# Linear attention and an ELU feed-forward layer on one core: the first two batches' k maxima by one strided reduction each pair of slots, the first batch's attention slot by slot, and new orders of work for the head and the first two blocks

## The chip, the core and the metric

The kernel runs on one core of one Trainium2 chip. The metric is the device time of one execution in microseconds (us). A core has a matrix engine (TensorE, PE in the profile; its weight loads are listed as PEld), a vector engine (VectorE, DVE), a scalar engine (ScalarE, ACT), a general one (GpSimd, POOL) and a queue engine (SyncE, SP) which here only issues transfers. Each engine works through its own instructions in the order in which the program wrote them, and waits on semaphores for the others.

## The reference

```
q_s = exp(q - max(q, axis=-1));  q_s /= sum(q_s, axis=-1)         # over the 64 columns of a row
k_s = exp(k - max(k, axis=2));   k_s /= sum(k_s, axis=2)          # over the 576 positions
kv  = einsum('bhsd,bhse->bhde', k_s, v)
att = einsum('bhsd,bhde->bhse', q_s, kv)
x   = att.transpose(0, 2, 1, 3).reshape(4608, 512)
h   = x @ w_in                                                    # 512 -> 2048
g   = where(h > 0, h, exp(min(h, 0)) - 1)
out = g @ w_out                                                   # 2048 -> 512
```

q, k and v have 8 batches, 8 heads, 576 positions and 64 columns, in float32.

## The kernel before

**Blocks and steps.** Block j (0 to 7) takes the feed-forward layer of 512 positions of batch j; the 64 positions that are left of each batch are gathered into a ninth block of 512. A block has 16 steps, one for each chunk of 128 of the 2048 hidden columns. A step issues `hidden` (four matmuls of 128x512, L912, then ACT's exponential L895 or, in some chunks, the clipped form L892 and L893, then POOL's affine step L896), then the projection (`project`, four matmuls L933 of the chunk three steps back, LAG = 3), then `elu` on DVE (L925). Hidden results use three PSUM banks in turn (the first four chunks use a fourth), the projection four others, and one bank (AB) is left for attention. So PE alternates four L912 and four L933.

**Attention as words.** While block j runs, the attention of batch j + 1 is done in small pieces. Each piece is a word; a table gives, for each step, three strings of words: behind `hidden`, behind `project`, behind `elu`. FIRST is the table of block 0, SECOND of block 1, LATER and CHANGED of the rest. What comes ahead of block 0, batch 0's whole attention with the first loads, is one string, START. The order in a string is the order in which instructions enter their engines' queues, and so an order written by hand. Words used below: `load:Q:1:A` (a transfer, on SP unless an engine is named), `qmax`, `qsub`, `qexp`, `qsum`, `qmul` (softmax of q: L672, L679, L684, L689/L691, L708), `kmax` (maximum of k over the positions that a partition holds, L326 in the first two batches), `kturn` and `kacross` (transposes by matmul and the maximum across partitions, L331, L358), `diag` and `kspread` or `kraw`/`kmin` (the maxima put on a diagonal by ACT, L368, and spread or subtracted by matmul, L465, L513, L524), `ksub` (L438), `kexp`, `vconv` (v to bf16), `kv` (L560), `kfac` (scale by the sums of k), `pturn`/`pwide` (transposes of q, L766, and their copy), `att`/`xc` (L805 and the copy into XT, the transposed input of block's hidden matmuls), `w1:a:b`, `w2:a:b` (weight chunks a to b-1, issued by POOL: L255, L262), `h` (hidden matmuls of block 0 in START), `warm` (matmuls of ones, L1093). `kout` and `kin` (L423) bring later batches' maxima through a scratch tensor in DRAM into NB, on ACT's queue. `hold` makes SP wait for the latest hidden matmul.

**Slots.** In batches 0 and 1 a slot is a pair of heads with nine rows of 64 columns in each partition (QN = 9); a slot's load of q, k or v has 288 KB, and there are four. `kmax_first` takes the maximum of the nine rows with four `tensor_tensor` instructions of DVE by way of KT2: rows 0 to 3 against 4 to 7, then 2 against 2, then 1 against 1, then row 8. `kturn_first`, `kacross_first` and what follows work on halves A (slots 0, 1) and B (2, 3); so do, in batch 0, `vconv_first`, `kv_first`, `kv_fac`, `qturn_slots` and `qwide_first`.

Keys of the semaphores are strings in `op`; a word waits for the writers of the keys that it reads.

Of the kernel before, what the change touches and what calls it, by code (L numbers as in the profile page):

```python
# [38 lines left out]
AT = {"rawA": 0, "rawA2": 1, "rawB": 7, "rawB2": 4, "rawS": 3, "rawT": 2,  # L39
      "kturnA": 4, "kturnB": 5, "kvA": 6, "kvB": 4, "pturnA": 5, "pturnB": 5,  # L40
      "att0": 6, "att1": 2, "att2": 3, "att3": 4, "clip": (1, 2, 4, 6, 8, 10, 11, 17, 21, 30, 32, 33, 37, 42, 44)}
START = ("load:Q:0:1 load:K:0:0 load:K:0:1 warm:1:7 warm:4:7 qmax:1 warm:2:4 load:Q:0:3 qsub:1:dve "
# [3 lines left out]
         "w1:4:6 kacross:B kexp:S vconv:A:act kmin:A qsub:2:gp qsub:3:gp diag:act:B w2:2:3 qsum:0 kmin:B "  # L46
         "kexp:A load:V:0:3 kmin:T qexp:2 qmul:A:dve qsum:2 load:V:0:2 qexp:3 w1:6:9 "
         "qsum:3 vconv:B:gp load:K:1:M qmul:2:gp kexp:B kexp:T kv:A kfac:A:dve pturn:A kv:B "
         "pwide:A:act kfac:B:act warm:1:3 att:1 att:0 qmul:3:gp pturn:B xc:1:dve xc:0 h:2:4 "
         "pwide:B:act w2:3:4 att:2 att:3 xc:2 load:Q:1:A load:Q:1:R w2:4:6 h:0:2 xc:3 kmax2:AB ")  # L50
FIRST = {
    0: ("qmax:A ksub:R:dve", "", "qsub:0:dve"),
    1: ("w1:13:14", "w1:9:12", "qsub:1:dve"),
    2: ("", "qmax0:R", "w2:6:9"),
    3: ("hold qexp:A", "load:Q:1:B:act", ""),
    4: ("w1:12:13", "w2:9:13", "load:K:1:R qsum:A qsub0:R:dve"),
    5: ("w1:14:16", "kturn", "kacross vconv:R qmax:C"),
    6: ("", "qmul:A hold", "load:V:1:RAB"),
    7: ("qexp0:R", "", "diag qsub:2:dve"),
    8: ("qsub:D", "kspread load:K:2:MR copy ksub:1 qsum0:R", "qexp:C qmulr0:dve ksub:0 qsum:C"),  # L60
    9: ("pturn:A", "", "ksub:3 kexp:R qmul:B:dve pwide:A:act"),
    10: ("", "pturn0:R pwide0:R:act", "ksub:2:dve vconv:A:gp"),
    11: ("rest0 rcopy0:act", "kexp:A", ""),
    12: ("pturn:B w2:15:16", "pwide:B:act load:Q:2:ABR", "w2:13:15"),
    13: ("kv:A vconv:B:dve", "kfac:A:dve", "kexp:B peak2:B att:0 xc:0"),
    14: ("kv:B kfac:B:dve peak2:R qmulr:gp", "att:1 peak2:A", "join2 turn:R xc:1"),
    15: ("att:3", "xc:3", "att:2 load:V:2:MR xc:2 kout2"),
}
SECOND = {
    0: ("qmax:C qsub:D", "", "qmax:A"),  # L70
    1: ("", "qsub:1 wide0:R:dve", ""),
    2: ("", "qsub:0 load:K:2:MR", ""),
    3: ("kin", "qsub:2 qexp:A", "qsum:A vconv:A:gp"),
    4: ("", "", "ksub:A"),
    5: ("rest0", "qexp:C", "peak2:B"),
    6: ("ksub:3:dve rcopy0:act vconv:B", "ksub:R:dve", "load:Q:2:MR"),
    7: ("", "kexp:A", "ksub:2 kexp:R"),
    8: ("qmul:1 qsum:C qmul:0:dve", "vconv:R", "kexp:B qmulr:dve"),
    9: ("turn:A", "qmul:B:dve", ""),
    10: ("peak2:R wide:A:gp kv:AB", "", ""),  # L80
    11: ("kfac:AB:dve", "turn:R turn:B qmax2:A", ""),
    12: ("peak2:A wide:R:act", "flat:0", "xflat:0:act"),
# [38 lines left out]
class Gen:  # L121
# [976 lines left out]
    def first_batch(self):  # L1098
# [7 lines left out]
        for word in START.split():  # L1106
# [101 lines left out]
```

## Time and profile before

| | us |
|---|---|
| time, median of 3 runs | 310.69 (310.32 to 311.09) |
| span of the profiled execution | 308.1 |
| PE busy | 297.6 (97%) |
| first L912 (hidden matmul) | 19.88 |
| first L933 (projection) of block 0 | 24.47 |
| of block 1 | 61.56 |
| of block 2 | 94.26 |
| of block 3 | 125.52 |

The times are of whole executions; the profile is of one execution, for which the page gives its span, 308.1 us, from the first to the last instruction. Times of events are counted from the span's start. The first L933 of a block is used as a mark, since PE alternates L912 and L933 from there on, and the distances between such marks show in which block time is spent.

### The profile page before, as it was taken

The numbers are of one execution on the slowest core, as the hardware profiler recorded it, in microseconds if no ns is written. First come the engines' busy times: TensorE is split into PE (matmuls) and PEld (weight loads), VectorE is DVE, ScalarE is ACT, GpSimd is POOL, SyncE is SP. The second block draws the span as 40 slices with busy tenths as digits, with TensorE's granted clock in tenths as the row PEclk, the third lists the DMA queues.
The fourth block names the chain that finished last, engine by engine and source line by source line (L and its number), as shares of the span: only waits on it lengthen the run. The fifth ranks groups of instructions, "written<-read, shape, count | busy, mean of one in ns | idle before, by whom it ended". The sixth has DMA issues, their size and how long they took to land.

```text
span 308.1 us, 4839 instructions
## 1 busy us (share of the span) xinstructions
PE 297.6 (97%) x1733; PEld 240.1 (78%) x1733; DVE 235.0 (76%) x400; ACT 192.9 (63%) x358; POOL 171.3 (56%) x215
## 2 busy tenths in 40 slices
PE   7789899999999999999999999999999999999995
PEld 4467677788878888888888888888888888888884
DVE  6988978979959897999889988998895353335442
ACT  2678975577559784877587758775877543334432
POOL 2968873686436743786278637863686333333440
PEclk9999999999999999999999999999999999999999
DMA  7999999985708993768475846590512030003004
GB/s 261 393 340 364 372 345 257 273 253 145 191 3 246 261 251 105 223 122 231 133 217 144 208 143 209 146 198 3 172 23 57 2 136 0 0 2 136 0 0 136
DMA packets 60584, 51.63 MB, mean 168 GB/s; under 512 B 26897, under 2 KB 50705, under 8 KB 60561
## 3 DMA queue, kind: packets, MB, share of 16 engines
q1 hardware_dynamic: 52960, 41.23, 47.7%
q0 software_dynamic: 6400, 8.39, 10.5%
q10 hardware_dynamic: 1200, 1.72, 2.0%
q8 instruction: 13, 0.21, 0.3%
q14 instruction: 11, 0.08, 0.1%
HBM read 38.27 MB, written 9.45 MB: 155 GB/s over the span
## 4 chain that ended last, share of the span: by engine, by line
PE 85%; DMA 6%; POOL 4%; ACT 2%; DVE 2%; issue 1%
PE bank L933 40%; PE bank L912 40%; DMA W2S<-in_moe_w_out_dram 5%; PE bank L827 2%; POOL W1S L255 1%; PE bank L598 1%; DMA QR<-in_q_dram 1%; POOL QR L679 1%; POOL QS L708 1%; PE bank L805 1%; DVE KT L326 1%; DVE QF L672 0%; PE bank L560 0%; ACT ES L895 0%; ACT ES L893 0%
## 5 line engine op out<-in xcount | busy, mean ns | idle before, releaser
L933 PE MATMUL bank<-W2S,GT 128*128 128x512 f32 x572 | 153.4, 391 | 1.4 <-DMA W2S<-in_moe_w_out_dram 1.2
L896 POOL TENSOR_SCALAR ES<-ES 128x512 f32<-128x512 f32 (+1 forms) x130 | 85.8, 662 | 117.3 <-ACT ES L895 117.3
L912 PE MATMUL bank<-XT,W1S 128*128 128x512 f32 x512 | 138.4, 392 | 0.5 <-issue 0.3
L925 DVE SCALAR_TENSOR_TENSOR GT<-bank,ES 128x512 fp32r<-128x512 f32 (+1 forms) x130 | 87.9, 681 | 54.4 <-PE bank L912 40.6
L933 PEld LDWEIGHTS bank<-W2S,GT 128*128 128x128 f32 x572 | 106.3, 188 | 23.6 <-DMA W2S<-in_moe_w_out_dram 1.6
L895 ACT ACTIVATE ES<-bank 128x512 f32<-128x512 f32 (+1 forms) x130 | 76.0, 592 | 70.9 <-PE bank L912 70.7
L912 PEld LDWEIGHTS bank<-XT,W1S 128*128 128x128 f32 x512 | 94.1, 188 | 19.9 <-ACT XT L814 0.9
L679 POOL TENSOR_TENSOR QR<-QR,QM 128x512 f32<-128x512 f32 (+1 forms) x21 | 24.9, 1187 | 0.6 <-DVE QM L672 0.5
L684 ACT ACTIVATE QR<-QR 128x1024 f32<-128x1024 f32 (+3 forms) x19 | 19.0, 1006 | 3.1 <-DVE QR L679 3.1
L855 ACT ACTIVATE XT<-bank 128x320 fp32r<-128x320 f32 (+1 forms) x30 | 15.0, 501 | 9.4 <-PE bank L827 9.3
L689 DVE TENSOR_REDUCE QZ<-QR 128x16 f32<-128x1024 f32 (+1 forms) x14 | 18.8, 1343 | 0.6 <-ACT QR L684 0.6
L672 DVE TENSOR_REDUCE QM<-QR 128x16 f32<-128x1024 f32 (+1 forms) x14 | 18.8, 1342 | 0.0
L912 PE MATMUL bank<-XTR,W1S 128*128 128x512 f32 x64 | 16.6, 389 | 0.0
L438 DVE TENSOR_TENSOR KR<-KR,NB 128x512 f32<-128x512 f32 x16 | 14.6, 938 | 0.0
L623 ACT ACTIVATE MB<-bank,KZ 64x64 fp32r<-64x64 f32 x44 | 10.1, 302 | 7.0 <-DVE KZ L614 6.9
L387 DVE TRANSPOSE_TENSOR_REDUCE KM<-KR 128x32 f32<-128x1024 f32 x12 | 14.4, 1226 | 0.0
L857 POOL CAST QT<-QW 128x1024 fp32r<-128x1024 f16 x12 | 12.5, 1039 | 2.9 <-DMA QW<-QS 2.9
L912 PEld LDWEIGHTS bank<-XTR,W1S 128*128 128x128 f32 x64 | 12.0, 188 | 2.5
L892 ACT ACTIVATE ES<-bank 128x512 f32<-128x512 f32 x15 | 8.9, 594 | 7.9 <-PE bank L912 7.9
L827 PE MATMUL bank<-QT,MB 128*128 128x320 f32 (+1 forms) x48 | 12.5, 300 | 0.7 <-ACT XT L855 0.7
L708 POOL TENSOR_TENSOR QS<-QR,QI 128x1024 f16<-128x1024 f32 (+1 forms) x7 | 12.5, 1783 | 0.4 <-DVE QI L691 0.4
L484 ACT ACTIVATE EK<-KR 128x1024 bf16<-128x1024 f32 x12 | 12.6, 1050 | 0.0
(108 smaller groups left out, 262.8 us busy)
## 6 DMA issues: line engine op xcount, KB each, us to landing
out_dram<-OSB SPq DMA_DIRECT2D x30, 256.0 KB, 2.7
KR<-in_k_dram SPq DMA_DIRECT2D x6, 1024.0 KB, 7.7
VR<-in_v_dram SPq DMA_DIRECT2D x6, 1024.0 KB, 6.3
QR<-in_q_dram SPq DMA_DIRECT2D x5, 1024.0 KB, 8.0
KR<-in_k_dram SPq DMA_DIRECT2D x8, 288.0 KB, 6.1
VR<-in_v_dram SPq DMA_DIRECT2D x8, 288.0 KB, 6.6
W1S<-in_moe_w_in_dram POOLq DMA_DIRECT2D x3, 768.0 KB, 9.2
QR<-in_q_dram SPq DMA_DIRECT2D x4, 512.0 KB, 11.2
```

The lines of the kernel that those rows point to most:

```text
L672: self.op("dve", lambda: v.tensor_reduce(m, QR, AX.X, ALU.max), self.qkeys(b, part), self.qstat("QM", b, part))
L679: self.op(en, lambda: e.tensor_tensor(QR, QR, m, ALU.subtract), keys + self.qstat("QM", b, part), self.qown(b, part))
L684: self.op("act", lambda: a.activation(QR, QR, AF.Exp), keys, self.qown(b, part))
L689: self.op("dve", lambda: v.tensor_reduce(z, QR, AX.X, ALU.add), self.qkeys(b, part), self.qstat("QZ", b, part))
L708: self.op(en, lambda: e.tensor_tensor(out, QR, z, ALU.mult), keys + self.qstat("QI", b, part), [f"QS{x}" for x in cells])
L827: last = pe.matmul(self.bank[bank][:, a - c0:b - c0], self.MB[f][:, :, :].rearrange("p u d -> p (u d)"), self.QT[:, f, a - f * S:b - f * S ...
L855: self.op("act", lambda: e.activation(out, src, AF.Copy), reads, writes)
L895: self.op("act", lambda: a.activation(ES[:, x], ps[:, x], AF.Exp), [f"bank{bank}"], keys + mark)
L896: self.op("gp", lambda: g.tensor_scalar(ES[:, x], ES[:, x], -1.0, 1.0, ALU.add, ALU.mult), keys, keys)
L912: return pe.matmul(ps, self.W1S[:, kc, c * 128:(c + 1) * 128], x[:, kc, 0:SM], start=(kc == 0), stop=(kc == 3))
L925: self.op("dve", lambda: v.scalar_tensor_tensor(out[:, x], *how), [f"bank{bank}"] + eks + (["FINE"] if n < FINE else []), keys)
L933: return pe.matmul(self.bank[OB[t]][:, :], self.GT[n % NG][:, t * 128:(t + 1) * 128], self.W2S[:, c, :], start=(c == 0), stop=(c == NCH - ...
```

## The change

Four parts:

1. `kmax_first` is one `tensor_reduce` (maximum over the innermost axis) on a view of k in which the nine rows are the innermost axis, with a step of 64 elements (256 bytes). One instruction takes two slots: 128x128 out of 128x1152. KT2 goes.
2. Batch 0 works per slot from q's product on: `vconv`, `kv`, `kfac`, `pturn`, `pwide` and `att` take a slot (0 to 3) or a half; the keys QT and VF are split by slot (`cells`, `slots`), and each slot has its own banks (`kv0` to `kv3`, `pturn0` to `pturn3`). `pwide` of a slot goes through the common `copy`.
3. START, FIRST and SECOND are written anew. In START the k loads come first, W1's chunks 0 to 3 are one transfer instead of two, all 16 hidden matmuls of the first four chunks are there, slice by slice (`h:kc:c0:c1`), and `hidden` issues none for them. Batch 1's q loads A and R go over POOL's queue instead of SP's. In FIRST, `kturn`, `kacross`, `diag`, `kspread` and `copy` stand in step 5 (before: steps 5 to 8). In SECOND, `kin` goes from step 3 to 4, and its first user, `ksub:A`, from POOL behind step 4 to DVE in step 5.
4. In `program`, the store of a finished block stands ahead of the words of that step, not behind them.

```diff
-START = ("load:Q:0:1 load:K:0:0 load:K:0:1 warm:1:7 warm:4:7 qmax:1 warm:2:4 load:Q:0:3 qsub:1:dve "
-         "load:Q:0:0 kmax:0 warm:3:5 load:K:0:2 kraw:A qexp:1 kmax:1 load:K:0:3 kturn:A load:V:0:1 "
-         "qmax:0 kraw:S qsum:1 qsub:0:gp kacross:A load:Q:0:2 kmax:3 kraw:B kmax:2 kmax2:R "
-         "load:V:0:0 w1:1:4 w1:0:1 diag:act:A qmax:2 kmin:S qexp:0 kraw:T kturn:B w2:0:2 qmax:3 "
-         "w1:4:6 kacross:B kexp:S vconv:A:act kmin:A qsub:2:gp qsub:3:gp diag:act:B w2:2:3 qsum:0 kmin:B "
-         "kexp:A load:V:0:3 kmin:T qexp:2 qmul:A:dve qsum:2 load:V:0:2 qexp:3 w1:6:9 "
-         "qsum:3 vconv:B:gp load:K:1:M qmul:2:gp kexp:B kexp:T kv:A kfac:A:dve pturn:A kv:B "
-         "pwide:A:act kfac:B:act warm:1:3 att:1 att:0 qmul:3:gp pturn:B xc:1:dve xc:0 h:2:4 "
-         "pwide:B:act w2:3:4 att:2 att:3 xc:2 load:Q:1:A load:Q:1:R w2:4:6 h:0:2 xc:3 kmax2:AB ")
+START = ("warm:10:2 load:K:0:1 load:K:0:0 load:Q:0:0 kmax:A kraw:S qmax:0 qsub:0:gp qexp:0 load:K:0:3 kturn:A kacross:A "
+         "w1:0:4 kraw:A load:K:0:2 load:Q:0:1 diag:dve:A load:Q:0:2 load:V:0:0 kmin:A kmax:B kmin:S kturn:B "
+         "load:Q:0:3 qmax:1 kexp:A vconv:0:act qmax:2 kraw:T kacross:B load:V:0:3 qsub:1:gp qmax:3 kexp:S "
+         "kraw:B load:V:0:1 qsub:2:gp qsum:0 diag:act:B qsub:3:gp qmul:0:gp kmin:T qexp:1 qsum:1 kv:0 "
+         "qexp:2 vconv:1:act qexp:3 qmul:1:gp kmin:B load:V:0:2 qsum:2 vconv:3:act qmul:2:dve kv:1 kexp:T "
+         "kexp:B w2:0:2 pturn:0 load:K:1:M pturn:1 vconv:2:gp kv:3 kfac:0:act kfac:1:act pturn:2 pwide:0:act "
+         "att:0 pwide:1:act kv:2 w1:4:6 att:1 qsum:3 kfac:3:act qmul:3:dve xc:0:dve pwide:2:act kfac:2:act "
+         "pturn:3 h:0:2:3 h:0:0:1 att:2 pwide:3:act xc:2:act h:0:1:2 xc:1:dve att:3 h:1:0:1 h:1:1:2 "
+         "load:Q:1:A:gp h:2:0:1 kmax2:AB w2:2:3 h:0:3:4 xc:3:act h:3:0:1 w1:6:9 h:1:2:3 h:2:1:2 w2:3:4 h:3:1:2 "
+         "h:2:2:3 h:3:2:3 h:1:3:4 h:2:3:4 h:3:3:4 load:Q:1:R:gp ")
 FIRST = {
-    0: ("qmax:A ksub:R:dve", "", "qsub:0:dve"),
-    1: ("w1:13:14", "w1:9:12", "qsub:1:dve"),
-    2: ("", "qmax0:R", "w2:6:9"),
-    3: ("hold qexp:A", "load:Q:1:B:act", ""),
-    4: ("w1:12:13", "w2:9:13", "load:K:1:R qsum:A qsub0:R:dve"),
-    5: ("w1:14:16", "kturn", "kacross vconv:R qmax:C"),
-    6: ("", "qmul:A hold", "load:V:1:RAB"),
-    7: ("qexp0:R", "", "diag qsub:2:dve"),
-    8: ("qsub:D", "kspread load:K:2:MR copy ksub:1 qsum0:R", "qexp:C qmulr0:dve ksub:0 qsum:C"),
-    9: ("pturn:A", "", "ksub:3 kexp:R qmul:B:dve pwide:A:act"),
...
+    0: ("qmax0:R", "", "w2:4:6"),
+    1: ("", "", ""),
+    2: ("qmax:A", "", "qsub0:R:gp"),
+    3: ("hold w1:9:12", "", ""),
+    4: ("", "qexp0:R", "w2:6:9"),
+    5: ("kturn kacross qsum0:R qsub:0:gp", "", "diag qsub:1:dve kspread load:Q:1:B:act qmax:C copy qexp:A qmulr0:gp qsub:2:dve w1:12:13"),
+    6: ("qsub:D", "pturn0:R", "qsum:A"),
+    7: ("pwide0:R:act ksub:0:dve w2:9:13", "", ""),
+    8: ("qexp:C rest0", "", "hold qmul:A"),
+    9: ("rcopy0:dve ksub:1:dve kexp:A", "pturn:A qsum:C pwide:A:act qmul:B:dve w1:13:14 load:V:1:RAB", "w1:14:16 qmulr:gp"),
...
 SECOND = {
-    0: ("qmax:C qsub:D", "", "qmax:A"),
-    1: ("", "qsub:1 wide0:R:dve", ""),
-    2: ("", "qsub:0 load:K:2:MR", ""),
-    3: ("kin", "qsub:2 qexp:A", "qsum:A vconv:A:gp"),
-    4: ("", "", "ksub:A"),
-    5: ("rest0", "qexp:C", "peak2:B"),
...
+    0: ("qmax:A qsub:1 qsub:0", "", ""),
+    1: ("", "", ""),
+    2: ("", "qmax:C", ""),
+    3: ("qexp:A", "qsub:2 qsub:D vconv:B", "qsum:A"),
+    4: ("kin", "qmul:0:gp", ""),
+    5: ("", "vconv:R wide0:R:act ksub:A:dve", "load:K:2:MR"),
...
@@ kmax_first
-        T = self.KT2[:, 4 * (x % 2):4 * (x % 2 + n), :].rearrange("p (u r) d -> p u r d", r=4)
-        steps = ((T, src[:, :, 0:4, :], src[:, :, 4:8, :], keys, kt), (
-            T[:, :, 0:2, :], T[:, :, 0:2, :], T[:, :, 2:4, :], kt, kt), (
-            T[:, :, 0, :], T[:, :, 0, :], T[:, :, 1, :], kt, kt), (
-            out, T[:, :, 0, :], src[:, :, 8, :], keys + kt, ka))
-        for o, p, q, reads, writes in steps:
-            self.op("dve", lambda: v.tensor_tensor(o, p, q, ALU.max), reads, writes)
+        src = self.KR[b][:, x * QN:(x + n) * QN, :].rearrange("p (u r) d -> p u d r", r=QN)
+        self.op("dve", lambda: v.tensor_reduce(self.KA[:, x:x + n, :], src, AX.X, ALU.max),
+                self.firstkeys("K", part, b=b), [f"KA{y}" for y in slots])
@@ hidden
-        self.hidden_mm(j, c, range(2, 4) if n < EARLY else range(4))
+        self.hidden_mm(j, c, () if n < EARLY else range(4))
@@ first_batch
             elif name == "h":
-                for c in range(int(args[0]), int(args[1])):
-                    self.hidden_mm(0, c, range(2))
+                for c in range(int(args[1]), int(args[2])):
+                    self.hidden_mm(0, c, (int(args[0]),))
@@ program
                 self.project(pj, ps)
-                self.do(j, end)
                 if ps == NCH - 1:
                     self.store(pj)
+                self.do(j, end)
```

More of the change, by code (lines that the diff above doesn't have):

```diff
@@ L86 @@
+    15: ("flat:5 xflat:5:act xrest:act join2", "", "kout2 qmax2:A"),
 }
@@ L148, in need, with cells, slots @@
                 know[s] = n
+    def cells(self, key):
+        if key in ("QTA", "QTB"):
+            return [f"QT{x}" for x in self.slots(key[-1])]
+        if key in ("VFA", "VFB"):
+            return [f"VC{x}" for x in self.slots(key[-1])]
+        return [key]
+    def slots(self, part):
+        return {"A": (0, 1), "B": (2, 3)}.get(part) or (int(part),)
     def op(self, en, fn, reads=(), writes=(), dma=None):
         own = f"s_{en}"
+        reads, writes = ([x for k in keys for x in self.cells(k)] for keys in (reads, writes))
         evs = []
@@ L618, in kv_fac @@
             sl, keys = slice(64 * u, 64 * u + 64), [f"MB{f}u{u}" for f in range(f0, f1)]
-            reads = [f"bank{bank}"] + [f"KZ{hh}" for hh in hs]
+            reads = [f"bank{bank}"] + [f"KZ{f}" for f in fs]
             if en == "act":
@@ L781, in qwide_first @@
         else:
[L782 to L783 removed]
+            xs = self.slots(part)
+            if len(xs) == 1:
+                u = xs[0] % 2
+                self.copy(en, self.QT[:, xs[0], 0:SM], ps[:, u * SM:(u + 1) * SM], [f"bank{bank}"], [f"QT{xs[0]}"])
+                return
+            out, key = self.QT[:, xs[0]:xs[0] + 2, 0:SM], f"QT{part}"
             src = ps[:, :].rearrange("p (j t) -> p j t", j=2)
[L785 to L788 removed]
+        self.copy(en, out, src, [f"bank{bank}"], [key])
     def qwide(self, part, en="act"):
```

99 lines of the change are left out of this document (45 added, 54 removed).

## The prediction

> **What bounds the kernel now.** I read the page's busy times first, then the chain of waits for the head, then the table of windows cut at the first L933 of blocks 0 to 3. The page:
>
> ```profile
> span 308.1 us, 4839 instructions
> PE 297.6 (97%) x1733; PEld 240.1 (78%) x1733; DVE 235.0 (76%) x400; ACT 192.9 (63%) x358; POOL 171.3 (56%) x215
> GB/s 261 393 340 364 372 345 257 273 253 145 191 3 246 261 251 105 223 122 231 133 217 144 208 143 209 146 198 3 172 23 57 2 136 0 0 2 136 0 0 136
> ```
>
> TensorE (PE) is busy for 97% of the span. So time can be won only where PE stands idle or does filler work. The windows say where (columns: stretch, length, then busy time and count of PE, weight loads, DVE, ACT, POOL, then granted clock, DMA share, GB/s):
>
> ```profile
> core 0: us, PE busy (x) PEld busy (x) DVE busy (x) ACT busy (x) POOL busy (x), PEclk, DMA share, GB/s
> 0.00:19.88 19.88, 14.98 (x176) 10.09 (x176) 16.48 (x48) 10.92 (x23) 13.28 (x24) 1.00 1.01 326
> 19.88:24.47 4.59, 4.44 (x18) 3.14 (x18) 4.33 (x11) 3.32 (x7) 1.25 (x4) 1.00 1.50 366
> 24.47:61.56 37.09, 35.62 (x237) 27.36 (x237) 32.74 (x56) 26.02 (x45) 25.24 (x28) 1.00 1.18 320
> 61.56:94.26 32.70, 32.01 (x181) 26.10 (x180) 27.24 (x46) 21.79 (x37) 19.58 (x23) 1.00 0.53 148
> 94.26:125.52 31.26, 31.26 (x177) 25.63 (x176) 27.21 (x45) 23.38 (x45) 17.66 (x21) 1.00 0.82 212
> ```
>
> In the block from 94.26 on PE has no idle time at all; the words of that block and of those behind it do not change, so whatever is won or lost earlier is carried to the end unchanged. Three stretches are open: the head up to the first hidden matmul (19.88), block 0 (1.47 idle of 37.09), and block 1 (0.69 idle of 32.70). The granted clock is 1.00 throughout. The chain of waits in the head (start, length, what):
>
> ```profile
> 5.10 0.35 DVE KT L326
> ...
> 7.46 0.69 DVE QF L672
> 8.15 0.07 issue
> 8.22 1.04 POOL QR L679
> 9.27 0.91 POOL W1S L255
> ...
> 16.88 2.01 POOL QS L708 x2
> ```
>
> On DVE the K maxima of two slots (5.10 to 7.46) sit in front of slot 0's row maximum (7.46), then POOL's subtraction (8.22), and only then may POOL issue the first piece of W1 (9.27).
>
> **The change part by part.** The span is 308.1 and the median of the runs 310.69; the 2.6 between them lies outside the span, and I carry it over unchanged.
>
> *Strided maximum, its cost.* Four instructions replace 24. The groups by form, and the reductions near them:
>
> ```profile
> L326 DVE TENSOR_TENSOR KT<-KT 128x128 f32<-128x128 f32 (+2 forms) x12 | 3.5, 292 | 0.4
> L326 DVE TENSOR_TENSOR KT<-KR 128x256 f32<-128x256 f32 (+1 forms) x6 | 3.1, 524 | 0.1
> L326 DVE TENSOR_TENSOR KA<-KT,KR 128x64 f32<-128x64 f32 (+1 forms) x6 | 1.5, 248 | 0.2
> L672 DVE TENSOR_REDUCE QM<-QR 128x20 f32<-128x1280 f32 x7 | 10.3, 1474 | 0.0
> L672 DVE TENSOR_REDUCE QM<-QR 128x16 f32<-128x1024 f32 x7 | 8.5, 1210 | 0.0
> L402 DVE TENSOR_REDUCE KC<-KM 128x16 f32<-128x80 f32 x6 | 1.3, 224 | 0.0
> L410 DVE TENSOR_REDUCE KQ<-KC 32x16 f32<-32x64 f32 x6 | 1.5, 252 | 0.2
> ```
>
> Removed: 3.5 + 3.1 + 1.5 = 8.1 us of DVE. Each new instruction reads 1152 elements per partition with a step of 256 bytes, which no row of before does. Dense, the slope between 1024 and 1280 elements is 264/256 = 1.03 ns per element, with about 0.14 fixed, so 1152 elements cost 1.33. The KC row reads with a step of 8 bytes and fits the same line (0.14 + 80 x 1.03 = 0.22). The KQ row reads with a step of 64 bytes and lies above it: (0.252 - 0.14)/64 = 1.75 ns per element, which over 1152 elements gives 2.1; its 0.04 excess may as well be fixed cost. Twice the dense slope would be 2.5. I take 1.33, since the rows hug the dense line, and keep 2.1 and 2.5 for the rivals; nothing suggests less than 1.33. Saved on DVE: 8.1 - 5.3 = 2.8 us, but DVE's time only counts where PE waits for it.
>
> [...]
>
> *The head.* The new string loads K slot 1, K slot 0, Q slot 0, in this order, on SP; issue times and landings of before's first transfers:
>
> ```profile
> 1.20 0.89 SPq L277 DMA_DIRECT2D KR<-in_k_dram  x2
> KR<-in_k_dram SPq DMA_DIRECT2D x1, 288.0 KB, 3.1
> KR<-in_k_dram SPq DMA_DIRECT2D x1, 288.0 KB, 4.1
> L672 DVE TENSOR_REDUCE QF<-QR 128x8 f32<-128x512 f32 x4 | 2.6, 681 | 1.0 <-DMA QR<-in_q_dram 1.0
> W1S<-in_moe_w_in_dram POOLq DMA_DIRECT2D x1, 768.0 KB, 9.2
> ```
>
> Position two lands at 1.20 + 3.1 = 4.3, position three (issued about 1.65) at 1.65 + 4.1 = 5.75. The maxima of slots 0 and 1 run from 4.3 to 5.65; slot 0's row maximum follows at 5.75 for 0.68, POOL's subtraction to 7.5, and W1 goes out there instead of at 9.27: 1.75 earlier. It is now one piece of 1024 KB instead of 768 and 256. The 768 took 9.2; another 256 KB at half of the page's 390 GB/s or so costs 1.3, alone 0.7. I take 1.3: landing 7.5 + 9.2 + 1.3 = 18.0. Attention per slot makes the other path shorter: the chain of before ended in two POOL products in a row (2.01) and the transposes behind them, whereas now each slot's products, transposes (16 at a time) and copy run while the next slot's are under way, and the last of PE's 64 transposes is no longer needed for the first hidden matmul. I put the first XT slot at 17.3 to 18.0, so W1 is the later, and the first hidden matmul at 18.3 rather than 19.88.
>
> From there to the first L933 the tail counts, and the pace of matmuls:
>
> ```profile
> 22.98 0.80 ACT L895 ACTIVATE ES<-bank 128x256 f32<-128x256 f32 x2 [0.59 <-PE bank L912]
> 27.32 1.07 PE L912 MATMUL bank<-XT,W1S 128*128 128x512 f32 x4
> 28.23 1.08 PE L933 MATMUL bank<-W2S,GT 128*128 128x512 f32 x4
> ```
>
> Four matmuls take 28.23 - 27.32 = 0.91, a step of eight 1.82. Chunk 0 needs 10 matmuls before its exponential (8 hidden ones, since those of other chunks stand between, and 2 of the attention): 2.3, and some 0.3 for the last XT slice. From its exponential to the first L933 it is 24.47 - 22.98 = 1.49, as now. First L933 at 18.3 + 2.6 + 1.49 = 22.4: **-2.0**. All 64 matmuls of the first four chunks are issued before hidden() now, but none is added. The number of warm matmuls before the hidden ones stays near (10 against 11), now all at the start on PE's idle time: nothing.
>
> *Weights in block 0.* PE now waits for W2 chunks 6 to 8 (a transfer of 768 KB, here with 0.95 at 37.57) and, shorter, for 9 to 12:
>
> ```profile
> PE bank L933 <- DMA W2S<-in_moe_w_out_dram: 1.2, 2, 0.9
> 37.57 0.73 PE L933 MATMUL bank<-W2S,GT 128*128 128x512 f32 x2 [0.95 <-DMA W2S<-in_moe_w_out_dram]
> W2S<-in_moe_w_out_dram POOLq DMA_DIRECT2D x1, 768.0 KB, 11.8
> ```
>
> Before, POOL's queue carries 5632 KB up to the end of W2 6:9 (landed 37.5); after, 6016, since batch 1's Q (512 + 128 KB) moves there from SP and one W1 piece of 256 moves behind. But SP carries V of batch 1 (1152 KB) and K and Q of batch 2 only later (hold at step 8 instead of 6, then 12 and 14). So what has to be moved until then is 6016 + 3456 (batch 0) + 1152 (K of batch 1) + 512 (last of its Q) = 11,136 KB. The page's first five slices moved 13,000 KB in 37 us, 353 KB per us; 11,136 takes 31.5 from 1.7, thus about 33 to 34. Chunk 6 is wanted six steps of 1.82 after the first L933 and after the new work in step 5: 22.4 + 10.9 + 1.6 = about 35. The wait goes: **-1.2**. If POOL's queue is slow by itself (5632 KB in 28.3 us, 199 per us), 6016 KB from 7.5 end at 37.7 and the wait grows to 2.5 (+1.2). I take the first, since the transfers share the DMA engines.
>
> *Batch 1's K maxima, all in step 5.* What ran in steps 5 to 8 with work in between now runs as one chain within one step:
>
> ```profile
> 31.79 0.41 DVE L358 TENSOR_REDUCE NM<-bank 128x4 f32<-128x256 f32 x1
> 33.12 1.27 ACT L368 ACTIVATE DG<-ID,NM 128x128 fp32r<-128x128 f32 x4
> 34.84 0.40 PE L465 MATMUL bank<-DG,HALF 128*128 128x256 f32 x2
> ```
>
> After its transposes PE has the four L933 of the step (0.91) and then stands in front of the L465 for DVE's 0.41, ACT's 1.27 and the handovers (about 0.2): 1.9 - 0.9 = **+1.0**, as nothing else is queued for PE there. Before, that wait did not exist.
>
> *Block 1.* The maxima's way back from DRAM:
>
> ```profile
> 61.76 0.35 ACTq L423 DMA_DIRECT2D NB<-kmax_scratch  x1
> NB<-kmax_scratch ACTq DMA_DIRECT2D x1, 256.0 KB, 3.6
> ```
>
> The word that issues it moves from step 3 to 4, its first user from POOL at the end of step 4 to DVE in step 5. Two steps are 3.6 us, about the transfer; with issue and queueing I expect DVE to wait 1.3. Behind it in DVE's queue stands the elu of step 5, for which the hidden matmul of step 8 waits (three banks). Three steps of slack cover most of it: **+0.2** (0 to +1.3). The other moves (V conversions, products and copies among ACT, POOL and DVE) have cover: block 1's DVE is busy 27.24 of 32.70, ACT 21.79, POOL 19.58. The store ahead of the words at step's end concerns evictions of 0.7 which come no later: nothing.
>
> Sum: -2.0 - 1.2 + 1.0 + 0.2 = -2.0. Span 306.1, time **308.7**.
>
> **The rivals.** *R1, the strided reduction is dear* (the other side). All four stand in DVE's one queue on the way to the first L933: two ahead of Q's row maxima, two (batch 1) ahead of the first elu. With a cost c the path grows by 4(c - 1.33), less the slack that I find: 0.1 before slot 0's Q lands, 0.7 before the next slots', 0.7 before the first elu, 1.5 in all. At 2.1 it is +1.6: 310.3, no change. At 2.5 it is +3.2: 311.9, slower. It breaks even at c = 2.2 and decides for slower by more than 0.93 from c = 2.45. For it: the KQ row; against: KC, and that KQ's 0.04 us may be fixed cost. [...]
> *R2, the way back from DRAM takes longer.* NB's row shows 3.6 with 148 GB/s on the DMA engines in block 1; a busier moment costs more, and once the slack is used each us beyond costs about one. At 5 us: +1.5, 310.2.
> *R3, weights come late.* By the POOL queue's own pace W2 brings +1.2 instead of -1.2: 311.1; if batch 1's K lands after 20 for the reductions ahead of the first elu, some tenths more.
>
> **How the numbers follow.** About 0.3%, or 0.93 us, is what a measurement of this kernel can tell from no change. Forecast .47 (own range 307.3 to 309.7: the head 0.7 and the wait in step 5 0.5 either way); R1 at 2.1 .14, R1 at 2.5 .26, R2 .07, R3 .06. Faster .47; same .14 + .11 = .25; slower .26 and .02 for R2 and R3 together: .28. The range runs from the forecast's lower end to R1's dear end, 307.3 to 312.0.
>
> **What would show it.** The reductions' row in the profile of the changed kernel: 1.33 right, 2.1 or 2.5 makes R1. W1's first issue near 7.5 and first L912 near 18.3; first L933 near 22.4; no wait of L933 for W2S; a wait of about 1.0 of L465 for ACT's DG; and the first L933 of block 1 about 59.4, of block 2 about 92.2. The prediction is wrong if the first L933 comes after 23.5, if the W2 wait stays, or if block 1 loses over a microsecond to NB.

## The result, and the profile after

The changed kernel takes 313.27 us (median of four, 312.80 to 314.53) against 310.50 for the kernel before in the same comparison: ratio 1.0103, 95% interval 1.0069 to 1.0137. It is slower by 1.0%, where the forecast was 0.6% faster. The profiled execution has a span of 311.0, 2.9 more than before.

The table of windows of the changed kernel, cut at the first hidden matmul and at the first projection of blocks 0 to 3 as in the prediction (columns: stretch, length, then busy time and count of PE, weight loads, DVE, ACT, POOL, then granted clock, DMA share, GB/s):

```profile
0.00:20.53 20.53, 15.90 (x175) 10.64 (x175) 15.92 (x35) 11.76 (x25) 12.64 (x23) 1.00 0.90 307
20.53:25.94 5.41, 4.96 (x25) 3.07 (x19) 5.41 (x6) 4.60 (x11) 4.11 (x8) 1.00 1.20 343
25.94:62.87 36.93, 35.36 (x236) 27.36 (x237) 30.40 (x51) 26.25 (x47) 25.05 (x29) 1.00 1.13 298
62.87:97.24 34.37, 32.40 (x181) 25.85 (x180) 28.87 (x45) 25.05 (x46) 19.06 (x24) 1.00 0.69 167
97.24:128.45 31.21, 31.21 (x177) 25.61 (x176) 27.08 (x45) 23.37 (x45) 17.46 (x21) 1.00 0.84 213
```

Against before: first hidden matmul 0.65 later, first projection 1.47 later, block 0 shorter by 0.16, block 1 longer by 1.67, block 2 the same (31.21 and 31.26). 1.47 - 0.16 + 1.67 - 0.05 = 2.93, the whole difference of the spans. The waits of PE (total, times, longest) and the reduction's row:

```profile
PE bank L835 <- POOL QT L865: 1.7, 2, 1.0
PE bank L469 <- DVE GT L933: 1.0, 1, 1.0
PE bank L813 <- DVE QS L714: 0.8, 1, 0.8
PE bank L774 <- ACT EK L537: 0.8, 1, 0.8
PE bank L335 <- DVE KA L329: 0.7, 1, 0.7
```

```profile
L329 DVE TENSOR_REDUCE KA<-KR 128x128 f32<-128x1152 f32 x4 | 8.7, 2186 | 1.7 <-DMA KR<-in_k_dram 1.7
```

No wait for W2 is left among PE's waits. In its place stand the spreading matmul of step 5 (L469 here, L465 before), the attention of the next batch in block 1 (words `flat`, L835) and waits in the head. The reduction costs 2.19 us, not 1.33; its four instructions take 8.7 us, 0.6 more than the 24 that they replace. The chain of waits of the head (start, length, what):

```profile
1.21 3.17 DMA KR<-in_k_dram
...
4.41 2.15 DVE KA L329
6.56 0.59 DVE QF L678
...
8.56 2.16 DVE KA L329
10.72 0.60 DVE QF L678
...
11.47 2.05 POOL QR L685 x2
13.52 0.02 issue
13.55 0.63 ACT QR L690
14.18 0.58 ACT VB L863
14.76 0.52 ACT QR L690
15.27 0.57 ACT VB L863
15.85 0.16 ACT EK L537
16.00 0.98 ACT EK L542 x2
...
20.88 3.78 DVE KA L329 x2
24.66 0.49 issue
25.15 0.40 DVE QF L678
25.55 0.34 DVE GT L933
```

Three times the chain runs through the reduction: ahead of the row maxima of slot 0 (4.41), of the other slots (8.56), and, for batch 1, ahead of the first elu (two reductions, 20.88 to 25.22 in the timeline; the chain books the last half microsecond of the second as issue). Between them ACT is the last: q's exponentials, V's conversions and k's exponentials stand one behind the other from 13.55 to 17.0. Behind that, PE waits 0.8 for a product on DVE (L813, QS in the list above). The first XT slot, which the first hidden matmul needs, is ready at 20.12; before it was 19.17.

### The profile page after: what moved, and what is told of

It reads as the page before. It is cut to its first block, busy times and chain, and to the rows that moved or that the text cites. A ratio compares the mean times of both kernels' runs of the same rounds, so it can differ in the third digit from the quotient of the medians.

```text
span 311.0 us, 4833 instructions
## 1 busy us (share of the span) xinstructions
PE 299.1 (96%) x1732; PEld 240.3 (77%) x1732; DVE 234.8 (75%) x376; ACT 198.6 (64%) x375; POOL 172.5 (55%) x220
## 3 DMA queue, kind: packets, MB, share of 16 engines
q10 hardware_dynamic: 1200, 1.72, 2.2%
## 4 chain that ended last, share of the span: by engine, by line
PE 81%; DVE 7%; DMA 5%; ACT 2%; POOL 2%; issue 1%; SPq 0%; DVEq 0%; ACTq 0%; POOLq 0%
PE bank L920 38%; PE bank L941 38%; DVE KA L329 3%; DMA VR<-in_v_dram 2%; PE bank L835 2%; DVE GT L933 2%; DMA QW<-QS 2%; DMA KR<-in_k_dram 1%; PE bank L604 1%; PE bank L813 1%; ACT VB L863 1%; DVE QS L714 1%; POOL QR L685 1%; POOL ES L904 1%; DVE QF L678 1%
## 5 line engine op out<-in xcount | busy, mean ns | idle before, releaser
L685 POOL TENSOR_TENSOR QR<-QR,QM 128x512 f32<-128x512 f32 (+1 forms) x22 | 26.3, 1203 | 2.6 <-DVE QM L678 2.6
L863 ACT ACTIVATE XT<-bank 128x320 fp32r<-128x320 f32 (+1 forms) x28 | 14.1, 505 | 11.0 <-PE bank L835 11.0
L629 ACT ACTIVATE MB<-bank,KZ 64x64 fp32r<-64x64 f32 x60 | 14.4, 303 | 7.2 <-DVE KZ L620 6.9
L442 DVE TENSOR_TENSOR KR<-KR,NB 128x512 f32<-128x512 f32 (+1 forms) x17 | 15.8, 955 | 0.2 <-DMA NB<-kmax_scratch 0.2
L865 POOL CAST QT<-QW 128x1024 fp32r<-128x1024 f16 x11 | 11.4, 1040 | 5.7 <-DMA QW<-QS 5.7
L835 PE MATMUL bank<-QT,MB 128*128 128x320 f32 (+1 forms) x48 | 12.6, 303 | 2.0 <-POOL QT L865 1.7
L714 POOL TENSOR_TENSOR QS<-QR,QI 128x1024 f16<-128x1024 f32 (+1 forms) x8 | 13.5, 1689 | 0.0
L835 PEld LDWEIGHTS bank<-QT,MB 128*128 128x128 f32 x48 | 8.9, 187 | 6.0 <-issue 2.5
L586 ACT ACTIVATE VB<-VR 128x1024 bf16<-128x1024 f32 x12 | 12.6, 1052 | 0.0
```

The lines of the kernel that those rows point to most:

```text
L685: self.op(en, lambda: e.tensor_tensor(QR, QR, m, ALU.subtract), keys + self.qstat("QM", b, part), self.qown(b, part))
L714: self.op(en, lambda: e.tensor_tensor(out, QR, z, ALU.mult), keys + self.qstat("QI", b, part), [f"QS{x}" for x in cells])
L835: last = pe.matmul(self.bank[bank][:, a - c0:b - c0], self.MB[f][:, :, :].rearrange("p u d -> p (u d)"), self.QT[:, f, a - f * S:b - f * S ...
L863: self.op("act", lambda: e.activation(out, src, AF.Copy), reads, writes)
```

## The experiments

Times are medians; a ratio is to the kernel before, run on the same chip. Marks are the first projection of blocks 0, 1 and 2, and a block's length is the distance between two marks.

**1. The reduction, undone in the changed kernel.** `kmax_first` and KT2 as before, every word as changed.

> The changed kernel with the four tensor_tensor steps back in place of each strided reduction, all words as changed. Two slots cost 0.69 + 0.42 + 0.29 + 0.29 = 1.70 us by the rows of before, against 2.19 by the row of the changed kernel. Theory A (the reduction is dear and stands on the path): first projection at 24.0 to 24.6 instead of 25.94, span 309.1 to 309.7. Rival (the new words of START set the head, ACT's and POOL's queues last): first projection still at 25.4 or later, span 310.4 or more. Block 1 as in the changed kernel, 34.4, by both.

312.94 over eight runs (311.19 to 313.89), ratio 1.0078 (1.0053 to 1.0103). First projection at 25.54, span 311.1: as it stands, this is the rival. But the granted clock of this profile is 0.78, 0.50 and 0.87 in the three windows from 18 to 24, where the profile of the changed kernel has 1.00. So this run alone cannot tell; experiment 5 repeats it.

**2 and 3. Block 1: the old table, and a swap on SP.**

```diff
-SECOND = { ... as changed ... }
+SECOND = { ... as before ... }
```

> The changed kernel with block 1's table as before. Theory (block 1's 1.67 us come from its new words): block 1 from first projection to first projection 32.7 instead of 34.37, head and block 0 unchanged (25.94; 36.9), span 309.3. Rival (block 1 loses because block 0 leaves its loads later, V, K and Q of batch 2 among them): block 1 stays above 33.8.

319.39, ratio 1.0297 (1.0271 to 1.0322): 6 us worse. Block 1 takes 38.97, with DVE waiting 4.2 for K of batch 3 and PE 2.9 behind it. The old table does not go with the rest of the change; why, experiments 8 and 9 show.

```diff
-    12: ("flat:2 xflat:2:dve load:Q:2:MR turn:B", ...
+    12: ("flat:2 xflat:2:dve turn:B load:Q:2:MR", ...
```

> The changed kernel with one swap: in step 12 of block 1, the transposes of q's second half go into SP's queue ahead of the load of batch 3's Q instead of behind it. If SP's order is the cause of the late second half: that cast on POOL starts at about 83.5 instead of 85.73, the waits of 0.68 and 0.30 at the flat attention go, block 1 33.4, span 310.0. If not, block 1 stays at 34.4. The wait of 1.0 for the rest's cast on POOL stays by both.

Block 1 falls to 32.88, and the cast of the second half starts at 84.36 in a block that began 1.45 later (64.32 instead of 62.87), so 20.0 behind the block's mark instead of 22.9. PE's waits of 0.68 and 0.30 are gone, and so is the 0.99 for the cast of the rest (the 64 left positions), which was expected to stay; why that one went is not known. The time stays (313.17, ratio 1.0092, 1.0056 to 1.0129), as the first projection of this profile comes at 27.49. The reason stands in its windows of the head (columns as above):

```profile
16.00:18.00 2.00, 1.28 (x66) 1.20 (x66) 1.12 (x6) 1.93 (x7) 2.00 (x3) 1.00 0.81 264
18.00:20.00 2.00, 1.16 (x22) 0.64 (x16) 1.18 (x3) 1.91 (x5) 2.00 (x4) 0.60 0.88 234
20.00:22.00 2.00, 2.00 (x32) 1.43 (x29) 1.45 (x4) 1.51 (x4) 2.00 (x4) 0.50 1.08 259
22.00:24.00 2.00, 2.00 (x6) 1.52 (x6) 2.00 (x2) 0.90 (x2) 0.93 (x2) 0.50 1.15 352
24.00:26.00 2.00, 2.00 (x8) 1.57 (x7) 2.00 (x2) 0.73 (x2) 0.00 (x0) 0.70 1.24 357
```

The column before the last two is the clock: from these means I estimate one half for about 6.8 us, from 18.4 to 25.2. START and the reduction are the same in the changed kernel's own profile, whose first projection is at 25.94 with a full clock; so the half clock goes with 1.55 us here. Experiment 2 has the same (27.52). The mean clock of the four runs of the changed kernel was 0.999, 0.995, 0.995 and 0.988, the last the slowest at 314.53; the kernel before had 0.998 to 1.000 in all of its runs. What this costs the whole kernel is not shown. Of the four runs of experiment 3 the one with the highest clock is the fastest (311.40 at 0.994, the others 312.89 to 313.85 at 0.989); but in experiment 1 the three runs at 1.000 took 311.19, 312.89 and 313.89, spread like the other five, and the changed kernel took 312.80 at 0.995 and 312.85 at 0.999.

**4. What the step between elements costs.** Eight reductions of 1152 elements to 128 in block 5 of the kernel before.

> The kernel before with eight added reductions in block 5, one in a step, each a maximum over nine elements with 128 results out of 1152 elements of a partition; only the step between the nine differs: 4, 8, 16, 32, 64, 128, 256 and 512 bytes. Their results are not used. [...] Rival (short rows of nine cost, whatever the step): 2.1 to 2.2 at 4 bytes too. A third (cost grows with the step): 256 and 512 bytes dearer than 32.

They took, by step in bytes: 4: 1.34, 8: 1.34, 16: 2.22, 32: 2.35, 64: 2.17, 128: 2.06, 256: 2.25, 512: 2.06. The timeline has the first three (4, 8, 16) as

```profile
185.31 1.34 DVE L1036 TENSOR_REDUCE KT<-W1S 128x128 f32<-128x1152 f32 x1
189.18 1.34 DVE L1036 TENSOR_REDUCE KT<-W1S 128x128 f32<-128x1152 f32 x1
201.58 2.22 DVE L1036 TENSOR_REDUCE KT<-W1S 128x128 f32<-128x1152 f32 x1
```

In this run the cost does not come of rows of nine (1.34 at 4 bytes), nor does it grow with the step: it jumps once, between 8 and 16 bytes, by 0.7 to 1.0 us, and stays. (One instruction for each step, in one run.) (The time of this run, 325.52, is of no use: the eight reductions add 15.8 us of work to DVE.)

**5. A full clock, and the reduction again.** Seven filler matmuls in the head's waits, then the four steps as well:

```diff
-... w2:0:2 pturn:0 load:K:1:M pturn:1 ... kfac:1:act pturn:2 pwide:0:act ...
+... w2:0:2 warm:2:5 pturn:0 load:K:1:M warm:2:5 pturn:1 ... kfac:1:act pturn:2 warm:3:5 pwide:0:act ...
```

> The changed kernel with seven more filler matmuls of 128x512 in the head's waits, two ahead of the transposes of slot 0, two ahead of those of slot 1, three ahead of the first attention matmul, in a bank that is free there. Theory C (the half clock between 18 and 25 us, which shows in three of four profiles of kernels with this START, comes of PE doing little there): granted clock 1.00 throughout in every run, first projection near 25.9, span 311.0 or less in each, median 0.5 to 1.0 under the changed kernel's. Rival (the dip comes by chance or from the total load): clock of the runs as mixed as before, 0.988 to 0.999, and the median the same or up to 0.5 higher.

> As the one with filler matmuls, and the four steps instead of the strided reduction. With the clock at 1.00 in both, the difference to that kernel is the reduction alone. Theory A: 1.0 to 1.5 us less, first projection 24.4 to 24.9. Theory C: under 0.5 us less.

With the filler the clock is 1.000 in all four runs, 312.71, ratio 1.0088 (1.0063 to 1.0113), about half a microsecond under the changed kernel's 313.27, within their spreads. One of the four took 314.04 all the same, so a full clock does not bring every run under the expected span. With the four steps 312.08 over eight, ratio 1.0054 (1.0036 to 1.0071); one of these eight has a clock of 0.994, so with the filler it can still fall. First projection 26.05 with the reduction, 24.71 with the four steps: in the changed START the reduction costs 1.34 up to there, as theory A says. But block 0 takes 37.25 and 38.34, and only 0.6 arrives at the end, between the sizes of the two theories, with intervals that overlap. What takes it back, by the timeline of the kernel with the four steps:

```profile
30.80 0.47 PE L479 MATMUL bank<-DG,HALF 128*128 128x256 f32 x2 [0.99 <-DVE GT L943]
40.23 0.61 PE L760 MATMUL bank<-ID,QS 128*128 128x128 f16 x8 [0.51 <-POOL QS L724]
44.31 0.62 PE L760 MATMUL bank<-ID,QS 128*128 128x128 f16 x8 [0.65 <-DVE QS L724]
```

The products of batch 1's q come later than PE asks for them, 0.51 and 0.65. With the reduction PE arrives there later, and the same transposes are listed without a wait.

**6. The reduction alone in the kernel before.**

> The kernel before with the strided reduction alone, all words as before. Its four single slots cost 1.18 each by the old steps and about 0.14 + 576 x 1.78 ns = 1.17 by the reduction; its two pairs (batch 1, ahead of the first elu) 1.70 and 2.19. Theory A (the reduction's price sets the head): +0.5 to +1.0 us, all by the first projection, 25.0 to 25.5. Theory C (what costs is the new order and the granted clock in the head, not the reduction): within 0.5 us of before, clock 1.00 up to 24 us.

309.90 over ten runs, ratio 0.9998 (0.9986 to 1.0009): no change. Its windows show why:

```profile
21.04:26.19 5.15, 4.47 (x18) 3.15 (x18) 5.15 (x5) 3.88 (x8) 1.56 (x4) 1.00 1.44 376
26.19:61.57 35.38, 35.16 (x236) 27.30 (x237) 32.72 (x56) 25.48 (x44) 24.98 (x27) 1.00 1.16 320
61.57:94.26 32.69, 32.00 (x182) 26.09 (x180) 27.57 (x46) 21.82 (x37) 19.68 (x23) 1.00 0.54 147
```

The first projection is 1.72 later than before, block 0 is 1.71 shorter, and block 1 begins at 61.57 as against 61.56. In the kernel before the head is covered by W2: PE arrives later, finds the weights there, and has lost nothing. (The waits for W2 are 1.2 of the 1.71; where the other half microsecond went was not traced. Nor is all of the 1.72 the reduction's: slot 0's row maximum comes 0.42 later in this profile, waiting for its load of q.)

**7. The tables of blocks 0 and 1 alone, then with the swap.** START, slots and reduction as before.

> The kernel before with the two new tables alone (blocks 0 and 1; W2's chunks 4 and 5 issued in step 0 as they ask). Theory D: first projection as before (24.5 to 25.5), then the 1.0 at the spreading matmul of step 5 and the waits at the flat attention of block 1: block 1 33.7 to 34.4, time 2 to 3 us over before. Rival: within 0.7 us of before.

> As the kernel with the new tables alone, with the transposes of q's second half ahead of the load in SP's queue in step 12 of block 1. Block 1 shorter by 0.7 to 1.5 (no wait for that cast on POOL), time 0.7 to 1.5 less, if SP's order is the cause; the same time if something else binds block 1.

313.06, ratio 1.0097 (1.0074 to 1.0121), the whole loss; with the swap 311.47, ratio 1.0048 (1.0027 to 1.0069). First projection 25.10 and 24.94, block 1 35.60 and 34.47. So the two tables alone lose as much as the change does, and the swap gives back 1.6 of it. That does not make START free: the losses of the parts do not add up to the whole, since the tables, by the medians, lose less with part 4 (experiment 10). New in both is a wait of the projection in step 3 of block 1 for the evictions (DVE's copies of finished projections out of their banks), 0.77 and 1.16:

```profile
60.83 1.48 DVE L672 TENSOR_REDUCE QM<-QR 128x20 f32<-128x1280 f32 x1
62.23 1.28 DVE L944 COPY OSB<-bank 128x512 f32<-128x512 f32 x2
```

The new table has the row maximum of 1.48 at the end of that step; with the store behind the words it stands ahead of the evictions on DVE. The store ahead of the words, which I had priced at nothing, keeps it behind them.

**8. START alone, with the store ahead of the words and behind them.** Tables as before, filler matmuls so that the clock stays; then also with the four steps.

> Only START, the slots and the reduction as changed (with the seven filler matmuls, so that the clock stays at 1.00); the tables of blocks 0 and 1 as before, W2's chunks 4 and 5 issued at START's end as they ask. Theory D (the new tables of blocks 0 and 1 are what costs): first projection at 25.5 to 26.2, block 0 shorter than 37.09 as W2 is no longer waited for, block 1 32.7, time within 0.6 us of before. Rival (the new START costs): 2 us or more over before.

> As the kernel with START alone, with the four steps instead of the strided reduction. If an earlier first projection is carried to the end: first projection 1.3 earlier (24.7) and the time 1.0 to 1.3 under that kernel's. If block 0's transfers and products take it back: first projection 24.7, block 0 longer by as much, time within 0.4.

> The kernel with START alone (filler matmuls, old tables), with the store behind the words of its step as before. Theory E (store ahead of the words puts batch 3's K load behind eight stores on SP): the wait of 5.7 us in block 1 goes, block 1 32.7 again; then the time shows START's own price: 0 to +1.5 over before, since the first projection is at 25.5 to 26.7 and block 0 can take back the wait for W2. If E is wrong, block 1 stays near 40.

With the store ahead: 319.66 (1.0307, 1.0277 to 1.0337) and with the four steps 318.58 (1.0273, 1.0244 to 1.0301), block 1 40.34 and 41.05. (The four steps bring 1.1 there, but the first projection only 0.54, at 26.20, so neither of the two expectations is met.) With the store behind the words: 311.60, ratio 1.0047 (1.0017 to 1.0077), block 1 32.69. Theory E holds. SP's queue, first in the kernel before, then in the first of the three:

```profile
55.31 0.61 SPq L293 DMA_DIRECT2D KR<-in_k_dram  x1
61.05 5.03 SPq L959 DMA_DIRECT2D out_dram<-OSB  x8
...
63.38 5.04 SPq L967 DMA_DIRECT2D out_dram<-OSB  x8
68.46 0.95 SPq L306 DMA_DIRECT2D KR<-in_k_dram  x1
```

Before, the same load of K is issued at 55.31, ahead of the first store (61.05). Eight stores, whose issue alone takes 5.04 and the first of which waits for the evictions, come in front of it, DVE waits 7.0 for K, and PE stands for 5.69; in that wait the granted clock falls (mean 0.62 from 76 to 80, 0.52 from 80 to 84). With the store behind the words START, with the slots and the reduction, costs 1.4 beside the old tables. The profile of that kernel is of its slowest run (313.29, median 311.60), and there the filler does not keep the clock (0.81 between 26 and 30): the first projection is at 27.84, as the row maximum of batch 1 waits 1.00 on DVE for q, which now comes over POOL's queue, and the first elu stands behind it. In the profile with the store ahead the same row maximum has no wait, and the first projection is at 26.74.

**9. The old table of block 1 again, with the store behind the words.**

> The changed kernel with block 1's table as before and the store behind the words as before. Theory E: block 1 32.7 to 33.2 instead of 38.97 (with the store ahead), so span 309.3 to 310.5 with the clock of the head as it falls. Rival (loads left late by block 0): block 1 over 34.

314.01, ratio 1.0129 (1.0097 to 1.0161). The store accounts for 4.75 of block 1 (34.22 instead of 38.97), but the 32.7 is not reached: a wait of 1.10 for the evictions remains. So the rival's bound, 34, is met too; block 1's old table fits block 0's new one badly even then, as with both tables old block 1 took 32.69 (experiment 8).

**10. The new tables, mended.** From the kernel with the tables and the swap: the store ahead; then the spreading matmul in step 6; then q's exponential behind the copy of the maxima.

```diff
-    5: ("kturn kacross qsum0:R qsub:0:gp", "", "diag qsub:1:dve kspread load:Q:1:B:act qmax:C copy qexp:A qmulr0:gp qsub:2:dve w1:12:13"),
-    6: ("qsub:D", "pturn0:R", "qsum:A"),
-    7: ("pwide0:R:act ksub:0:dve w2:9:13", "", ""),
+    5: ("kturn kacross qsum0:R qsub:0:gp", "", "diag qsub:1:dve load:Q:1:B:act qmax:C qmulr0:gp qsub:2:dve w1:12:13"),
+    6: ("kspread copy qexp:A qsub:D", "", "qsum:A"),
+    7: ("pturn0:R ksub:0:dve w2:9:13", "pwide0:R:act", ""),
```

> The kernel before with the new tables, the swap in step 12 of block 1, and the store ahead of the words. The wait of 0.8 to 1.2 of the projection for the evictions in step 3 of block 1 goes, as the row maximum of 1.48 no longer stands ahead of them on DVE: 0.8 to 1.2 less than with the swap alone (311.47), 310.3 to 310.7. If the stores' issue on SP delays a load that block 1 needs: no gain.

> As the last, with the spreading matmul and its copy behind the hidden matmuls of step 6 and the rest's transposes behind those of step 7. The wait of 0.99 in step 5 goes if nothing comes in its place: 309.3 to 309.7, some 0.6 under before. If ACT's copy or the subtractions come late instead: 310.3 or more, with a new wait at the rest's transposes or later.

> As the kernel with the spreading in step 6, with q's exponential behind the copy of the maxima on ACT. The wait of 1.00 goes and nothing takes it back: 309.2 to 309.7, block 0 36.0, 0.5 to 1.0 under before. If the products of q's first half come late for their transposes instead (0.5 or more in step 9): within 0.3 of before.

310.80 (1.0035, 1.0010 to 1.0059), 310.39 (1.0012, 0.9997 to 1.0027) and 309.42 (0.9983, 0.9971 to 0.9995; twelve runs). The last beats both kernels, the one before by 0.41 us, with an interval just clear of 1 and less than the 0.5 to 1.0 expected. Of the 0.8 to 1.2 expected of the first, 0.67 came, and its interval overlaps that of the swap alone. In the second the wait of 1.00 only moved to the rest's transposes, which need the bank that ACT's copy empties; that copy stood behind an exponential of 1.06. With the copy first it goes, block 0 takes 36.06 and block 1 32.79.

The first of the three has everything that the kernel of experiment 3 has, except START, the slots and the reduction: 310.80 (1.0035) against 313.17 (1.0092). So beside the new tables these cost 1.8 us by the ratios, 2.4 by the medians.

An earlier try moved the spreading matmul alone, in the changed kernel with filler and swap:

> As the one with filler matmuls, with the transposes of q's second half ahead of the load in block 1, and with the spreading matmul of batch 1's maxima moved from the end of step 5 to behind the hidden matmuls of step 6. If the terms are separate: block 1 32.9 instead of 34.4 (-1.5), the wait of 1.0 of that matmul for the step's elu gone, so block 0 about 35.9; span 308.5. If the wait of step 5 only moves on (W2's chunks 6 to 8 or the bank of attention come next): block 0 stays above 36.6, span 309.5.

313.27, ratio 1.0093 (1.0071 to 1.0114): block 1 32.51 as expected, but block 0 38.32, with this wait of PE for the same copy in place of the 1.0:

```profile
PE bank L774 <- ACT NB L475: 1.9, 1, 1.9
```

**11. The reduction where nothing covers it.** The best kernel with the strided reduction.

> As the last, with the strided reduction in place of the four steps. Theory F (in the kernel before, the reduction's price was hidden by block 0's wait for W2; here that wait is gone): first projection 0.5 to 1.7 later, time 0.5 to 1.0 more than the last. Rival (block 0 takes it back in other ways, as with the filler and the four steps): within 0.3 of the last.

311.07, ratio 1.0032 (1.0016 to 1.0048): 1.65 more than with the four steps, first projection 26.65 instead of 24.78. The same exchange that is free in the kernel before costs 1.65 here, more than the 0.5 to 1.0 that theory F gave it. The clock falls in this profile (0.89, 0.50 and 0.75 from 18 to 24, 1.00 in the other), but it does not account for the cost: nine of the twelve runs have a mean clock of 0.998 or more, and their median is 311.03. Nor do the two dearer reductions alone (0.49 each); the rest was not taken apart.

## Why the prediction was wrong, point by point

The span was forecast at 306.1 and is 311.0. Of the 4.9 between them the head has 3.5 (forecast -2.0, measured +1.47) and block 1 has 1.5 (forecast +0.2, measured +1.67). So the steps that failed are the head's -2.0, with the reduction priced at 1.33 and the first XT slot put early without a row, and block 1's +0.2, where SP's queue was not followed. Block 0 came out as forecast.

*The reduction's cost: the row was misread.* Of 1.33, 2.1 and 2.5 I took the first; it is 2.19. The KQ row (1.75 ns per element at 64 bytes) was the nearest row in kind and gave 2.1. I set it aside as fixed cost. This was R1 at 2.1 in its size, to which I gave .14. For 2.5, twice the dense slope, there was no row, and no run shows it: the dearest step took 2.35. Experiment 4 shows that the step was the cause, not a fixed cost: 1.34 at 4 and 8 bytes, 2.06 to 2.35 from 16 to 512.

*The head, -2.0: it came out at +1.47.* Three terms of it failed. W1 went out at 8.29 rather than 7.5, since the first reduction takes 2.15; it landed at 18.5 instead of 18.0, so this term was nearly right and not the last. The first XT slot was put at 17.3 to 18.0 without a row. It was ready at 20.12; by the chain above ACT works through exponentials and V's conversions in series, and the second reduction stands ahead of them. And from the first hidden matmul to the first projection it took 5.41, not 4.1: batch 1's reductions end at 25.22, and the elu waits. R1 had priced that as 4(c - 1.33) less 1.5, which at 2.19 gives +1.9 on a head of -2.0, about even with before. The remaining 1.5 no rival had. It is not the reduction's: with the four steps and the filler (experiment 5) the first XT slot is still ready only at 19.43 and the first projection comes at 24.71, 0.24 behind the kernel before instead of some 2 ahead. I read it from the chain as ACT's series, with DVE's product behind it; no run of its own took that apart.

*The granted clock: left out.* "Nothing" for the warm matmuls did not ask about the clock. Their number is 10 instead of 11, and the one that went stood late, just ahead of the attention; between 14 and 20 PE now does little but small matmuls with waits between (3.76 us busy of the 6, before 4.78). In the profiles of experiments 1 to 3 the clock then falls to 0.50; the first projection came 1.55 later in the one that can be compared. PE's longest wait between the first filler and the fall was 0.84 in these three; in experiment 8 the clock fell, by an estimate from the means given there, some 2.5 us into the wait of 5.69. In the profiled execution of the changed kernel it did not fall, so the 2.9 of the spans has no part of it. With seven matmuls in those waits it stayed at 1.000 in the four runs, and with the four steps as well at 0.999 or more in seven of eight. What brings the fall is not shown: the missing matmul, the small work and the waits were not tried apart.

*The wait for W2, -1.2: it went, with both times behind it off.* With step 5's +1.0 it makes -0.2 for block 0, and block 0 is 0.16 shorter. But W2 6:9, issued at 28.73, landed at 36.8, not 33 to 34, and PE asked for chunk 6 at 39.68, not near 35:

```profile
28.73 0.75 POOL L275 DMA_DIRECT2D W2S<-in_moe_w_out_dram  x1
W2S<-in_moe_w_out_dram POOLq DMA_DIRECT2D x1, 768.0 KB, 8.1
```

The landing came about 3 us later than forecast and the asking nearly 5, so that the size came out is partly luck. PE's late arrival is not what ended the wait: with the new tables under the old START PE is earlier and does not wait for W2 6:9 either (landed at 35.54 and wanted at 38.85 with the tables alone; 35.03 and 37.59 in the best kernel, whose first projection is at 24.78). So it was the new table of block 0; which of its moves did it was not tried. In the kernel before, the head and the weights are one term, the later of two: the reduction alone costs 1.72 in the head and nothing at the end. In the changed kernel no such wait stands behind the head, and block 0 took back no more than 0.16 of its +1.47.

*Step 5, +1.0: right.* 1.00 at 32.05 in the timeline. It is put down to the elu of the step, which ends at 31.97; ACT's last piece of the diagonal, which the working had as the cause, ends at 31.91, so the two end together.

*Block 1, +0.2: it was +1.67.* NB cost no more than was said (DVE waits 0.2 for it, where 1.3 was expected and mostly covered). What was missed is the other half of the table, which I covered with three busy shares. SP carries the transposes of q's second half, and the new words put three pieces of batch 3's Q ahead of them:

```profile
77.97 0.58 SPq L306 DMA_DIRECT2D QR<-in_q_dram  x1
78.60 1.61 SPq L298 DMA_DIRECT2D QR<-in_q_dram  x2
80.25 2.27 SPq L732 DMA_TRANSPOSE QW<-QS  x1
...
85.73 1.04 POOL L865 CAST QT<-QW 128x1024 fp32r<-128x1024 f16 x1 [3.08 <-DMA QW<-QS]
...
81.80 0.38 PE L835 MATMUL bank<-QT,MB 128*128 128x320 f32 x1 [0.99 <-POOL QT L865]
86.91 0.38 PE L835 MATMUL bank<-QT,MB 128*128 128x320 f32 x1 [0.68 <-POOL QT L865]
```

From issue to the cast it is 5.5 us, with POOL waiting 3.08 and PE behind it (86.91). With the two words swapped the transposes go out at 79.43, 15.1 behind the block's mark instead of 17.4, and the cast starts 4.9 after that. Block 1 lost 1.5 less in experiment 3 and 1.1 less in experiment 7. The other wait (81.80) is for the cast of the rest, behind transposes of its own; with the swap it went in experiment 3, but 0.90 of it stayed in experiment 7, so its cause stays open.

*The store ahead of the words: priced at nothing.* With the old table it costs 4.75 us of block 1, with the new one it ends an eviction wait of 0.8 to 1.2 (0.67 by the medians, with intervals that overlap). It belongs to the table.

*The rivals.* R1 was right that the reduction is dear, with .40 of the chance, but not in the outcome: at 2.19 it gives 310.6, and the measured time is 2.7 above that. R2 did not happen, R3 only in W2's landing. The outcome lies above the range because the wrong terms all went one way, and because ACT's series in the head and SP's order in block 1 had no row in my working.

*Slips in the working.* The first four chunks have 16 hidden matmuls, not 64; nothing hung on it. Five slices of the page are 38.5 us, not 37, which makes 338 KB per us and a landing of W2 at about 34.6 instead of 33 to 34. And the 2.6 between span and median is not all outside the span: runs that list both have 1.75 to 2.22 between them, so the profiled execution was faster than the median.

## What to carry to other kernels

Where two things end last by turns, as the head's work and the weights' transfers in the kernel before, a gain in one is worth the smaller of it and the other's slack; so ask of each saving what else arrives at the same place, and of each cost whether a wait already covers it. An exchange that measures as free in one order of work can cost its full price in another (0.0 and 1.65 us here), so it has to be tried in the order in which it will stand. And of a rewritten order every queue must be followed word by word, the one that only issues transfers first: here loads put ahead of a transpose cost 1.1 to 1.5 us of a block, eight stores ahead of a load 4.75.

## What the hardware showed

In experiment 4 a maximum by one instruction on float32, 128x128 out of 128x1152, took 1.34 us at a step of 4 and of 8 bytes and 2.06 to 2.35 us at steps of 16 to 512 bytes. With 0.14 fixed, the estimate from the rows of 1024 and 1280 elements in the prediction, that makes about 1.0 and 1.7 to 1.9 ns for each element. In experiment 3 TensorE's granted clock fell to one half, for 6.8 us by the estimate from its windows, in a head in which, from the first filler to the fall, it stood idle for no more than 0.84 us at a time; the kernel before has waits of 0.84 and 0.85 in its head and no fall in its profile. With seven more matmuls of 128x512 in the head of the changed kernel the mean clock was 1.000 in four runs out of four, without them 0.988 to 0.999.
